# Two chained matmuls per expert: computing the first one also by quarters in seven products, with the sums of its input kept in DRAM

## The chip, the cores and the metric

The kernel runs on 1 core of one Trainium2 chip. The metric is device time in microseconds (us). Before the change it took 1112.87 us (median of 3 runs, 1112.77 to 1113.21). Every run below that is called fast ran at a mean granted TensorE clock of 0.98 or more in its records. Single runs, whose state cannot be told, are marked.

Engines: PE is TensorE (PEld: its weight loads, which overlap its matmuls: 693.4 us of loads beside 1072.2 us of matmuls in the 1108.5 us of the kernel before), DVE is VectorE, ACT is ScalarE, POOL is GpSimd, SP issues DMA transfers (POOL issues some of them too). The order of each engine's instructions is laid down when the kernel is built, and the traces show the engines keeping to it (in a run below ACT did 19 operations in a row, 11.75 us, while PE waited for one behind them). The program keeps a plan of operations with estimated durations, orders them, and issues them engine by engine.

## The reference, cut to what matters

```python
def _attn_ref(q, k, v, w_phi):     # a linear attention; 8 x 8 heads of 576 rows, 64 wide
    ...
def _moe_ref(x, w_gate, w1, w2):   # x: 4608 x 512, 8 experts, F = 1024
    P = np.exp(x @ w_gate - max)
    for _ in range(8):             # routing: normalise rows and columns in turn, 8 times
        P /= P.sum(1, keepdims=True) + 1e-09
        P /= P.sum(0, keepdims=True) + 1e-09
        P *= N / E
    for e in range(E):
        h = np.maximum(x @ w1[e], 0.0)      # "up":   512 -> 1024
        out += P[:, e:e+1] * (h @ w2[e])    # "down": 1024 -> 512
    return out
```

The rows of x are worked on in 9 groups of 512. Expert 0 is computed beside the attention and the routing, because its products need no `P`. Experts 1 to 7 follow: 63 expert-groups of one up and one down.

## The kernel before

Down of experts 1 to 7 is already computed by quarters. Each matrix is cut into 2 x 2 blocks, and the block product is formed from seven block products instead of eight, at the price of sums of blocks. Four sums of the activations (`S`) are made for every group, two on POOL and two on DVE. Four sums of the weights (`T`) are made once per expert on POOL.

```python
def up(w1, g, hT, fcs, n, r=(), w=()):           # plain: 8 blocks of four 512-column matmuls
    for f0 in fcs[::n]:
        ph = new(f"P{n}")
        ...   pe(512, ... mm(ph..., w1()[:, dc, f*128:(f+1)*128], xT[:, dc, g*512:(g+1)*512], ...))
        act(512 * n, ... nc.scalar.activation(out=hT..., in_=ph..., func=ACT.Relu ...))

def sums_w(w2):                                  # once per expert, on POOL
    T = new("T")
    for n, x, y, r in ((0, b[0,1], b[0,0], []), (1, b[1,1], lambda: t(0), [0]), ...):
        pool(1024, lambda: nc.gpsimd.tensor_tensor(out=t(n), in0=x(), in1=y(), op=ALU.subtract), ...)

def down7(e, g, hT, w2, T):
    add(pool, 2, lambda: a(0, 0), lambda: a(1, 0), ALU.subtract, hk[0])     # S sums of a group
    add(dve,  0, lambda: a(1, 0), lambda: a(1, 1), ALU.add, ...)
    add(dve,  1, lambda: S[0](), lambda: a(0, 0), ALU.subtract, ...)
    add(pool, 3, lambda: a(0, 1), lambda: S[1](), ALU.subtract, ...)
    ...                                          # seven products of eight 256-column matmuls
    if e == 1:                                   # expert 0's share of acc gets its gate value
        for ts in range(4):
            act(512, ... nc.scalar.activation(out=acc[g][:, ts, :], in_=acc[g][:, ts, :],
                func=ACT.Copy, scale=P[:, 4*g + ts, 0:1]), ...)
    # six products are read by DVE:          acc = P_e * bank + acc   (two per product)
    # one is scaled by ACT into U and added by POOL:  acc = acc + U

for e in range(1, E):
    w1, w2 = load_w(e, ...)
    T = sums_w(w2)
    for g in ...:
        hT = new("hT"); up(w1, g, hT, ...); down7(e, g, hT, w2, T)
```

Of the kernel before, what the change touches and what calls it, by code (L numbers as in the profile page):

```python
# [41 lines left out]
class Op:  # L42
    __slots__ = ("eng", "dur", "lat", "nbytes", "fn", "left", "ready", "users", "idx", "end",
                 "bufs", "deps")
# [8 lines left out]
class Plan:  # L53
# [3 lines left out]
    def __init__(self):  # L57
        self.last, self.readers = {}, {}
        self.ops = []
        self.prio = 0  # L60

    def op(self, eng, dur, lat, fn, r=(), w=(), takes=(), nbytes=0):

        o = Op()
        o.eng, o.dur, o.lat, o.fn, o.nbytes = eng, dur, lat, fn, nbytes
        o.users, o.idx, o.end, o.ready = [], len(self.ops) + self.prio, None, 0.0
        deps = {}
        for key in r:
            for d in self.last.get(key, ()):
                deps[id(d)] = d  # L70
        for key in w:
            for d in list(self.last.get(key, ())) + self.readers.get(key, []):
                deps[id(d)] = d
        bufs = list(takes)
        for key in list(r) + list(w):
            b = key[0] if isinstance(key, tuple) else key
            if isinstance(b, Buf):
                bufs.append(b)
        o.bufs = list({id(b): b for b in bufs}.values())
        for b in o.bufs:  # L80
            b.left += 1
        for key in r:
            self.readers.setdefault(key, []).append(o)
        for key in w:
            self.last[key] = [o]
            self.readers[key] = []
        o.deps = list(deps.values())
        o.left = len(o.deps)
        for d in o.deps:
            d.users.append(o)  # L90
        self.ops.append(o)
        return o

    def start(self, o, free):

        t = max(free, o.ready)
# [11 lines left out]
    def schedule(self):  # L108
# [7 lines left out]
        while len(done) < len(self.ops):  # L116
# [17 lines left out]
            free[o.eng] = at + o.dur  # L134
            if o.nbytes:
# [27 lines left out]
def kernel(  # L163
# [33 lines left out]
    ps = ctx.enter_context(tc.tile_pool(name="ps", bufs=1, space=PSUM))  # L197

    ident = const.tile([128, 128], BF16, name="ident")
    wphi_f = const.tile([128, DF], FP32, name="wphi_f")  # L200
    wphi2 = const.tile([128, 2, DF], BF16, name="wphi2")
    wphi2f = wphi2.rearrange("p a b -> p (a b)")
# [9 lines left out]
    a_in = tc.alloc_tile_pool(name="a_in", bufs=1)  # L212

# [15 lines left out]
    def dve(el, fn, r=(), w=()):  # L229
        plan.op("DVE", el / 960.0 + 0.09, 0.22, fn, r, w)  # L230

    def pool(el, fn, r=(), w=()):
        plan.op("POOL", el * 1.64e-3 + 0.17, 0.25, fn, r, w)
# [13 lines left out]
    ring(hp, [128, 8, 512], BF16, "hT", 2)  # L247
# [22 lines left out]
    ring("s_p", [128, 4, 4, 256], BF16, "T", 2)  # L270
    ring("s_p", [128, 4, 256], BF16, "S", 8)
    ring("s_p", [128, 2, 256], FP32, "U", 2)
    ring("s_p", [128, NT, E], FP32, "u", 1)
    ring("s_p", [128, NT, E], FP32, "wv", 1)
# [14 lines left out]
    def load_w(e, r=()):  # L289
        w1, w2 = new("w1"), new("w2")  # L290
        dma("POOL", 2 << 20, 280, lambda: nc.gpsimd.dma_start(  # L291
            out=w1(), in_=moe_w1[e].rearrange("(c p) f -> p c f", p=128)),
            r, [(w1, i) for i in range(4)])
        dma("POOL", 2 << 20, 280, lambda: nc.gpsimd.dma_start(
            out=w2(), in_=moe_w2[e].rearrange("(c p) f -> p c f", p=128)),
            r, [(w2, i) for i in range(4)])
# [350 lines left out]
    def up(w1, g, hT, fcs, n, r=(), w=()):  # L647

        for f0 in fcs[::n]:
            ph = new(f"P{n}")  # L650
            for i in range(n):
                for dc in range(NP):
# [3 lines left out]
                        xkeys(g, dc) + [(w1, (f0 + i) // 2), *r], [ph, *w], [hT])  # L656
            act(512 * n, lambda f0=f0, ph=ph: nc.scalar.activation(  # L657
                out=hT()[:, f0:f0 + n, :].rearrange("p a b -> p (a b)"),
                in_=ph()[:, 0:512 * n], func=ACT.Relu, bias=0.0, scale=1.0),
                [ph], [(hT, f0 + i) for i in range(n)])  # L660

    def down(w2, hT, tss, r=()):
        py = new(f"P{len(tss)}")
        for i, ts in enumerate(tss):
            for fc in range(8):
                pe(512, lambda i=i, ts=ts, fc=fc: mm(
                    py()[:, 512 * i:512 * i + 512], hT()[:, fc, ts * 128:(ts + 1) * 128],
                    w2()[:, fc, :], fc == 0, fc == 7),
                    [(hT, f) for f in (range(8) if fc == 0 else (fc,))]
# [8 lines left out]
    def up0(g, part):  # L678
        if part == 0:
            hts[g] = new("hT")  # L680
# [53 lines left out]
    LAG = 6  # L734
# [82 lines left out]

    def routing():
        c_bc = None
        for it in range(8):  # L820
            rr, wv, cs, pc = new("rr"), new("wv"), new("cs"), new("P1")
# [5 lines left out]
            else:  # L827
                u = new("u")
                uk = [u]
# [7 lines left out]
                out=wv(), in0=L, in1=rr()[:, :, None].to_broadcast([128, NT, E]),  # L837
                op=ALU.mult), lk + [rr], [wv])
            dve(480, lambda wv=wv, cs=cs: nc.vector.tensor_reduce(
                out=cs(), in_=wv().transpose([0, 2, 1]), axis=AX.X, op=ALU.add), [wv], [cs])  # L840
# [6 lines left out]
            out=P, in0=wv(), in1=c()[:, None, :].to_broadcast([128, NT, E]), op=ALU.mult),  # L847
# [22 lines left out]
    def sums_w(w2):  # L870

        b = {(i, j): (lambda i=i, j=j: w2()[:, 4 * i:4 * i + 4, 256 * j:256 * j + 256])
             for i in range(2) for j in range(2)}
        T = new("T")

        def t(n):
            return T()[:, n]

        wk = [(w2, i) for i in range(4)]
        for n, x, y, r in ((0, b[0, 1], b[0, 0], []), (1, b[1, 1], lambda: t(0), [0]),  # L880
                           (2, b[1, 1], b[0, 1], []), (3, b[1, 0], lambda: t(1), [1])):
            pool(1024, lambda n=n, x=x, y=y: nc.gpsimd.tensor_tensor(
                out=t(n), in0=x(), in1=y(), op=ALU.subtract),
                wk + ["late"] + [(T, i) for i in r], [(T, n)])
        return T

    def down7(e, g, hT, w2, T):



        def a(i, j):
            return hT()[:, 4 * j:4 * j + 4, 256 * i:256 * i + 256]

        def b(i, j):
            return w2()[:, 4 * i:4 * i + 4, 256 * j:256 * j + 256]

        S = [new("S") for _ in range(4)]
        hk = [[(hT, f) for f in range(4 * j, 4 * j + 4)] for j in range(2)]
        wk = [(w2, i) for i in range(4)]

        def add(eng, n, x, y, op, r):
            f = nc.vector if eng is dve else nc.gpsimd
            eng(512 if eng is dve else 1024,
                lambda: f.tensor_tensor(out=S[n](), in0=x(), in1=y(), op=op), r, [S[n]])  # L904

        add(pool, 2, lambda: a(0, 0), lambda: a(1, 0), ALU.subtract, hk[0])
        add(dve, 0, lambda: a(1, 0), lambda: a(1, 1), ALU.add, hk[0] + hk[1])
        add(dve, 1, lambda: S[0](), lambda: a(0, 0), ALU.subtract, [S[0]] + hk[0])
        add(pool, 3, lambda: a(0, 1), lambda: S[1](), ALU.subtract, [S[1]] + hk[1])

        def product(bank, lhs, rhs, r, first):
            for i in range(2):
                for k in range(4):
                    z = i == 0 and k == 0
                    pe(256, lambda i=i, k=k, z=z: nc.tensor.matmul(  # L915
                        bank()[:, 256 * i:256 * i + 256], lhsT=lhs()[:, k, 128 * i:128 * i + 128],
                        rhs=rhs()[:, k, :], start=first and z, stop=k == 3,
                        skip_group_check=True), r + wk + (["P"] if z else []), [bank])
# [10 lines left out]

        if e == 1:  # L930
# [6 lines left out]
        product(y, lambda: a(0, 1), lambda: b(1, 0), hk[1], True)  # L937
        read(y, 0, 0)
        product(x, lambda: a(0, 0), lambda: b(0, 0), hk[0], True)
        u = new("U")  # L940
        for n in range(2):
            act(256, lambda n=n: nc.scalar.activation(
                out=u()[:, n, :], in_=x()[:, 256 * n:256 * n + 256], func=ACT.Copy, bias=0.0,
                scale=P[:, 4 * g + n, e:e + 1]), [x, "P"], [(u, n)])
        pool(512, lambda: nc.gpsimd.tensor_tensor(  # L945
            out=acc[g][:, 0:2, 0:256], in0=acc[g][:, 0:2, 0:256], in1=u(), op=ALU.add),
            [(u, 0), (u, 1)], [("acc", g, n, 0) for n in range(2)])
        product(z, lambda: S[0](), lambda: T()[:, 0], [S[0], (T, 0)], True)
        read(z, 1, 1)
        product(x, lambda: S[1](), lambda: T()[:, 1], [S[1], (T, 1)], False)  # L950
        read(x, 0, 1)
        product(x, lambda: S[2](), lambda: T()[:, 2], [S[2], (T, 2)], False)
        read(x, 1, 1)
        product(z, lambda: S[3](), lambda: b(1, 1), [S[3]], False)
        read(z, 0, 1)
        product(x, lambda: a(1, 1), lambda: T()[:, 3], hk[1] + [(T, 3)], False)
        read(x, 1, 0)

    for e in range(1, E):
        w1, w2 = load_w(e, [("xT", 5, 3)])  # L960
        T = sums_w(w2)
        for g in (list(range(NG)) if e < E - 1 else [8] + list(range(8))):
            hT = new("hT")
            up(w1, g, hT, range(8), 1, r=["up0"])
            plan.prio = 100
            down7(e, g, hT, w2, T)
            plan.prio = 0
            if e == E - 1:
                for ts in range(4):
                    store(g, ts)  # L970
    plan.run(tc)
# [30 lines left out]
```

## Time and profile before

| what | value | view |
|---|---|---|
| profiled span | 1108.5 us, clock 0.995 | cores |
| PE busy | 97% | page, part 1 |
| share of PE in the chain that ended last | 86% | page, part 4 |
| period of a middle group | 13.02 us, PE busy throughout | windows |
| an expert of nine groups (experts 2 to 6) | 118.0 to 118.3 us | timeline |
| up of a group | 8 x 0.867 = 6.93 us | timeline |
| down of a group | 7 x 0.868 = 6.08 us | timeline |

These lines of the page before give the busy time of each engine with its share of the span and number of instructions, and the shares of the chain of work that ended last.

```profile
PE 1072.2 (97%) x8024; PEld 693.4 (63%) x8024; DVE 637.6 (58%) x1422; ACT 579.9 (52%) x1190; POOL 565.1 (51%) x520
...
PE 86%; ACT 5%; DVE 4%; issue 1%; POOL 0%; DVEq 0%; ACTq 0%
```

The windows view of the kernel before, over two periods of a middle group, lists the stretch, its length, busy time and number of instructions of PE, PEld, DVE, ACT and POOL, the granted clock, the DMA share and GB/s.

```profile
599.70:612.72 13.02, 13.02 (x90) 8.62 (x89) 6.35 (x15) 5.61 (x11) 5.46 (x3) 1.00 0.00 1
612.72:625.74 13.02, 13.02 (x90) 8.60 (x89) 6.36 (x15) 5.61 (x11) 6.27 (x4) 1.00 0.22 35
```

PE is busy for the whole period, and DVE, ACT and POOL for less than half of it. A change here is worth what it takes from PE, as long as the other engines keep up.

The PE timeline of the kernel before (start, length, engine, line, operation, number) shows two up blocks and two down products.

```profile
601.58 1.03 PE L379 MATMUL P_8440<-xT,w_6228 128*128 128x512 bf16 x4
602.44 1.03 PE L379 MATMUL P_8448<-xT,w_6228 128*128 128x512 bf16 x4
...
609.26 1.04 PE L915 MATMUL P_8408<-w_6457,S 128*128 128x256 bf16 x8
610.13 1.04 PE L915 MATMUL P_8366<-T,S 128*128 128x256 bf16 x8
```

Blocks overlap in this view (1.03 us long, but 0.86 us apart), so the spacing of starts is what counts: 0.86 us for four 512-column matmuls (about 216 ns each) and 0.87 for eight 256-column ones (108.5 ns).

The timeline of the kernel before at an expert boundary (DVE and POOL) shows the one thing that disturbs it there.

```profile
543.15 2.11 POOL L882 TENSOR_TENSOR T<-w_7654 128x1024 bf16<-128x1024 bf16 x1
543.68 2.13 DVE L904 TENSOR_TENSOR S<-hT 128x1024 bf16<-128x1024 bf16 x1
545.23 2.56 POOL L882 TENSOR_TENSOR T<-w_7654,T 128x1024 bf16<-128x1024 bf16 x1
```

The DVE sum, which takes 0.68 us when nothing disturbs it, took 2.13 us while POOL summed weights. This cost PE a wait of 0.66 us. It recurs every 118 us, and is the boundary cost of the kernel before.

### The profile page before, as it was taken

To read this page: it belongs to the slowest core of one execution; us is meant where nothing else is said; L and a number is where in the kernel's file an instruction comes from. 1 tells how busy PE (TensorE), PEld (TensorE's weight loads), DVE (VectorE), ACT (ScalarE), POOL (GpSimd) and SP (SyncE) were. 2 spreads that over 40 slices of the span, in tenths; PEclk is the share of its full clock that TensorE was granted. 3 is DMA by queue.
4 is the path that set the end of the run, shared out by engine and by line. 5 is a ranking of instruction groups with operands and counts; after the bars stand their busy time and mean duration, and the time that the engine had idled before them with its cause. 6 is when DMAs were issued, how large, how long until landed. Compare 5 with 4: busy or idle time off the path is not lost.

```text
span 1108.5 us, 20141 instructions
## 1 busy us (share of the span) xinstructions
PE 1072.2 (97%) x8024; PEld 693.4 (63%) x8024; DVE 637.6 (58%) x1422; ACT 579.9 (52%) x1190; POOL 565.1 (51%) x520
## 2 busy tenths in 40 slices
PE   5889999999999999999999999999999999999997
PEld 3556666644566666666666666666666666666665
DVE  6889888883445555444545555444545555444455
ACT  6799899927744444444444444444444444444442
POOL 8775655530743447444743474445644474444433
PEclk9999999999999999999999999999999999999999
DMA  9997978402100040002200220022000400002112
GB/s 157 154 175 117 152 127 153 70 1 47 31 1 1 5 73 1 1 1 40 38 1 1 39 39 1 1 39 38 1 1 2 75 2 1 1 1 76 77 77 114
DMA packets 84189, 53.52 MB, mean 48 GB/s; under 512 B 43008, under 2 KB 77952, under 8 KB 84096
## 3 DMA queue, kind: packets, MB, share of 16 engines
q0 software_dynamic: 40080, 26.23, 17.6%
q1 hardware_dynamic: 44016, 26.02, 10.0%
q8 instruction: 62, 1.02, 0.4%
q14 instruction: 31, 0.25, 0.1%
HBM read 61.95 MB, written 9.44 MB: 64 GB/s over the span
## 4 chain that ended last, share of the span: by engine, by line
PE 86%; ACT 5%; DVE 4%; issue 1%; POOL 0%; DVEq 0%; ACTq 0%
DVE acc_79 L924 1%; ACT hT L657 1%; DVE S L904 1%; PE P_5334 L915 0%; PE P_13295 L915 0%; PE P_13027 L915 0%; PE P_10496 L915 0%; PE P_9961 L915 0%; PE P_7970 L915 0%; PE P_6773 L915 0%; PE P_6238 L915 0%; PE P_12759 L915 0%; PE P_12625 L915 0%; PE P_12353 L915 0%; PE P_12221 L915 0%
## 5 line engine op out<-in xcount | busy, mean ns | idle before, releaser
L904 POOL TENSOR_TENSOR S<-hT,S 128x1024 bf16<-128x1024 bf16 x63 | 133.9, 2125 | 284.8 <-DVE S L904 284.8
L915 PEld LDWEIGHTS <-S 128*128 128x128 bf16 x2016 | 197.5, 98 | 38.3 <-issue 1.4
L904 POOL TENSOR_TENSOR S<-hT 128x1024 bf16<-128x1024 bf16 x63 | 133.5, 2118 | 102.2 <-ACT hT L657 102.2
L915 PEld LDWEIGHTS <-hT 128*128 128x128 bf16 x1512 | 148.1, 98 | 25.2 <-issue 5.6
L904 DVE TENSOR_TENSOR S<-hT 128x1024 bf16<-128x1024 bf16 x63 | 51.9, 824 | 14.0 <-ACT hT L657 14.0
L379 PEld LDWEIGHTS <-w_3836 128*128 128x128 bf16 x288 | 28.2, 98 | 32.3
L379 PEld LDWEIGHTS <-w_11016 128*128 128x128 bf16 x288 | 28.2, 98 | 32.0
L379 PEld LDWEIGHTS <-w_7425 128*128 128x128 bf16 x288 | 28.2, 98 | 32.1
L379 PEld LDWEIGHTS <-w_6228 128*128 128x128 bf16 x288 | 28.2, 98 | 32.1
L379 PEld LDWEIGHTS <-w_9819 128*128 128x128 bf16 x288 | 28.2, 98 | 32.1
L379 PEld LDWEIGHTS <-w_8622 128*128 128x128 bf16 x288 | 28.1, 98 | 32.1
L379 PEld LDWEIGHTS <-w_5074 128*128 128x128 bf16 x288 | 28.1, 98 | 32.1
L904 DVE TENSOR_TENSOR S<-S,hT 128x1024 bf16<-128x1024 bf16 x63 | 47.6, 756 | 0.0
L379 PEld LDWEIGHTS <-hT 128*128 128x128 bf16 x288 | 28.1, 101 | 26.3 <-issue 2.3
L379 PEld LDWEIGHTS <-w_429 128*128 128x128 bf16 x288 | 25.8, 98 | 23.5 <-issue 2.1
L379 PEld LDWEIGHTS <-qkT 128*128 128x128 bf16 x256 | 23.5, 98 | 17.6 <-DVE xb_r L590 4.2
L291 POOL DMA_DIRECT2D w_5074<-in_moe_w_dram x1 | 0.8, 823 | 29.0 <-PE P_5064 L379 29.0
L319 POOL DMA_DIRECT2D qk<-in_k_dram x17 | 13.5, 795 | 2.2 <-issue 1.1
L319 POOL DMA_DIRECT2D qk<-in_q_dram x17 | 13.0, 767 | 0.0
L604 PEld LDWEIGHTS <-xb 128*128 128x128 bf16 x128 | 8.0, 97 | 3.4 <-issue 1.7
L945 POOL TENSOR_TENSOR acc_78<-acc_78,U 128x512 f32<-128x512 f32 x7 | 9.3, 1330 | 0.0
L452 PEld LDWEIGHTS <-qk 128*128 128x128 bf16 x64 | 4.5, 102 | 7.5 <-DMA qk<-in_k_dram 4.9
(3730 smaller groups left out, 2979.2 us busy)
## 6 DMA issues: line engine op xcount, KB each, us to landing
v_m<-in_v_dram SPq DMA_DIRECT2D x15, 512.0 KB, 5.1
qk<-in_k_dram POOLq DMA_DIRECT2D x15, 256.0 KB, 5.5
qk<-in_q_dram POOLq DMA_DIRECT2D x15, 256.0 KB, 6.2
w_429<-in_moe_w_dram POOLq DMA_DIRECT2D x4, 256.0 KB, 7.0
w_988<-in_moe_w_dram POOLq DMA_DIRECT2D x4, 256.0 KB, 9.2
w_3836<-in_moe_w_dram POOLq DMA_DIRECT2D x1, 1024.0 KB, 10.7
w_3851<-in_moe_w_dram POOLq DMA_DIRECT2D x1, 1024.0 KB, 16.5
w_5074<-in_moe_w_dram POOLq DMA_DIRECT2D x1, 1024.0 KB, 8.1
```

The lines of the kernel that those rows point to most:

```text
L291: dma("POOL", 2 << 20, 280, lambda: nc.gpsimd.dma_start(out=w1(), in_=moe_w1[e].rearrange("(c p) f -> p c f", p=128)), r, [(w1, i) for i i ...
L319: dma("POOL", nh << 17, 230, lambda x=x, src=src: nc.gpsimd.dma_start(out=t["qk"]()[:, x, o:o + nh], in_=src[b, hh:hh + nh, 0:SM].rearrang ...
L379: nc.tensor.matmul(out_, lhsT=lhsT, rhs=rhs, start=start, stop=stop)
L452: pe(128, lambda x=x, c=c, ptr=ptr: nc.tensor.transpose(bf(ptr)[:, c * 128:(c + 1) * 128], t["qk"]()[:, x, h0 + c // 2, (c % 2) * 128:(c % ...
L604: pe(128, lambda j=j: nc.tensor.transpose(bf(pxt)[:, j * 128:j * 128 + 128], xb()[:, j, :], ident), [(xb, 0), (xb, 1), "ident"], [pxt])
L657: act(512 * n, lambda f0=f0, ph=ph: nc.scalar.activation(out=hT()[:, f0:f0 + n, :].rearrange("p a b -> p (a b)"), in_=ph()[:, 0:512 * n], ...
L904: lambda: f.tensor_tensor(out=S[n](), in0=x(), in1=y(), op=op), r, [S[n]])
L915: pe(256, lambda i=i, k=k, z=z: nc.tensor.matmul(bank()[:, 256 * i:256 * i + 256], lhsT=lhs()[:, k, 128 * i:128 * i + 128], rhs=rhs()[:, k ...
L924: dve(350, lambda n=n, ts=ts: nc.vector.scalar_tensor_tensor(out=acc[g][:, ts, 256 * j:256 * j + 256], in0=bank()[:, 256 * n:256 * n + 256 ...
L945: pool(512, lambda: nc.gpsimd.tensor_tensor(out=acc[g][:, 0:2, 0:256], in0=acc[g][:, 0:2, 0:256], in1=u(), op=ALU.add), [(u, 0), (u, 1)], ...
```

## The change

The intent is to save an eighth of the up matmuls as well. Up becomes 7 block products for each of two halves of the features, 14 products of four 256-column matmuls: 56 x 108.5 ns = 6.08 us instead of 6.93. In return:

- Four more weight sums per expert (eight in all) run on POOL. Two of them are made in place in the weight buffer.
- Sums of xT are needed in every group of every expert. They are computed once, in expert 1, stored to DRAM, and loaded for each group (two transfers of 256 KB).
- Up results are now sums of several banks: ACT copies a bank to SBUF (`U`), and DVE adds another bank to it with a saturating add that also does the relu. There are six such adds a group, where ACT alone did the relu before.
- To make room on DVE, four products per group go through ACT and POOL instead of one; in return all four `S` sums go to DVE.
- The order of the products of up (of this group) and down (of the last group) is written out and fixed. Buffers and `LAG` (6 to 7) are adapted.

```diff
@@ sums of the weights: eight instead of four, on POOL @@
-    def sums_w(w2):
+    def sums_w(w1, w2):
+        sub(pool, 1024, s(2), q(w1, *a11), q(w1, *a21), ALU.subtract, ... + late, [S[2]])
+        sub(pool, 1024, q(w1, *a21), q(w1, *a21), q(w1, *a22), ALU.add, ...)      # in place
+        sub(pool, 1024, s(1), q(w1, *a21), q(w1, *a11), ALU.subtract, ...)
+        sub(pool, 1024, s(3), q(w1, *a12), s(1), ALU.subtract, ...)
+        ...  # the same four for w2
@@ sums of xT: computed once, kept in DRAM @@
+    def sums_x(g):
+        X = [new("X") for _ in range(2)]
+        ...  sub(dve, 512, x(n), y, z, ALU.subtract, ...)                          # four
+        for i in range(2):
+            dma("SP", 1 << 18, 250, lambda i=i: nc.sync.dma_start(out=Xd[g][i], in_=X[i]()), ...)
+    def load_x(g):
+        ...  dma("SP", 1 << 18, 250, lambda i=i: nc.sync.dma_start(out=X[i](), in_=Xd[g][i]), ...)
@@ up by quarters @@
+    def up7(A, g, X, hT, r0):
+        def keep(fp, n):   act(512, lambda: nc.scalar.copy(out=u[fp][n]()..., in_=x[fp]()), ...)
+        def add(bank, fp, n, i, j):
+            dve(660, lambda: nc.vector._custom_dve(ADD_SAT, out=out_(fp, i, j),
+                in0=bank[fp]()..., in1=u[fp][n](), s0=3.0e38, s1=0.0), ...)
+        ...  # x1 y1 x2 w1 x3 x4 w2, each for fp = 0 and 1
@@ down7: all S sums on DVE; four products through ACT and POOL @@
-        add(pool, 2, ...)   add(pool, 3, ...)
+        sub(dve, 1024, lambda: S[2](), ...)   sub(dve, 1024, lambda: S[3](), ...)
+        def read2(bank, i, j):
+            ...  act(256, ... scale=P...)  twice;  pool(512, ... acc = acc + u)
@@ the loop @@
+    ORDER = "X1 x10 x11 y11 w11 x21 x20 w10 x31 y10 w21 x30 X2 x41 x40 Z1 X3 w20 X4 Z2 Y1".split()
     for e in range(1, E):
         w1, w2 = load_w(e, [("xT", 5, 3)])
-        T = sums_w(w2)
+        if e == 1:
+            for g in range(NG):
+                sums_x(g)
+        A7, B7 = sums_w(w1, w2)
         for g in ...:
+            X = load_x(g)
+            ...  # the products of ORDER: up7 of this group, down7 of the last one
```

## The prediction

> **What bounds the kernel now.** The page gives PE 97% of 1108.5 us; the chain of waits is 86% PE. In the timeline the expert phase (63 expert-groups, about 272 to 1100 us) repeats every 13.0 us without gaps: 8 up blocks of four 512-column matmuls, 0.867 us each (6.93), then 7 down products of eight 256-column matmuls, 0.868 us each (6.08). Windows over one period: PE 13.00, DVE 6.3, ACT 5.6, POOL 5.5 us. Long chain entries recur every 118.0 us, so an expert boundary costs 118.0 - 9 x 13.0 = about 1 us (a DVE sum of 2.1 to 2.5 us). Attention and routing hardly change.
>
> **What the change removes.** Up becomes 14 products of four 256-column matmuls: 56 x 108.5 ns = 6.08 us instead of 6.93. That is 0.86 us per group, 54 us in all. The weight load (98 ns) stays hidden below 108.5 ns. All of it is on the critical path while PE stays gap-free.
>
> **What it adds per group,** from durations of the trace:
> - DVE: six PSUM adds of 128x512 (estimate 0.7 us, from 0.68 us for PSUM copies of 512) = 4.2; four sums instead of two, 4 x 0.68 = 2.7; six accumulates x 0.44 = 2.6. Sum 9.5 of 12.15 us.
> - ACT: 8 x 0.60 + 8 x 0.42 = 8.2 us.
> - POOL: four f32 adds x 1.27 = 5.1 us; its two sums of 2.12 go to DVE.
> - DMA: 512 KB of x sums, some 43 GB/s, on nearly idle queues.
>
> So PE still bounds a steady group, in a tight order with DVE near 80%. I expect 0.1 to 0.4 us of PE waits per group, nearer the first.
>
> **Where the gain is lost.**
> 1. Expert boundaries. POOL does eight weight sums (2.12 to 2.4 us each) instead of four. In its in-order queue they stand between the adds, and one waits for a weight load of 8 to 10 us: about 16 us of POOL work in a 12 us group. [...]I expect 2 to 5 us per boundary, six boundaries: 20 us.
> 2. Expert 1 computes, stores and reloads the x sums through three shared buffers: 4 us. Routing's multiplications, slowed by the POOL sums, hide under expert 0.
> 3. The first group has no down product beside it, the last no up: 3 us.
>
> Sum: -54 + 6 (steady waits) + 14 (boundaries, beyond today's 6) + 4 + 3 = -27 us.
>
> **Prediction: 1086 us,** 8 in 10 between 1060 and 1107. Faster by over 2%: 0.66; within 2%: 0.30; slower: 0.04.
>
> **What would show each step.** Right: a middle group's period of 12.2 to 12.5 us in the timeline; expert matmuls (1 to 7) of 256 columns; DVE 75 to 85% busy in such a window; adds of 0.7 us; 112 to 116 us from expert to expert, with PE gaps in the groups around each boundary that end on POOL weight sums, or on ACT or DVE behind them. Wrong: 12.8 or more in middle groups, with PE waiting for "hT", "U" or bank reads.
>
> **What would make it wrong.** The custom add at half rate (DVE over 12 us, no gain); POOL adds and DVE sums blocking each other in every group; x loads late behind stores in the SP queue; or, to the other side, boundaries as smooth as today (about 1065).

The trace of before does show DVE sums of 2.1 to 2.5 us beside POOL's weight sums, where they take 0.68 us alone.

## The result, and the profile after

The changed kernel is correct and took 1095.61 us (median of 4 fast runs, 1094.63 to 1095.97) against 1112.82 us for the kernel before (4 fast runs, 1112.63 to 1113.21). The ratio is 0.984, 95% interval 0.983 to 0.986. Ratios here are the mean time of one kernel's fast runs over that of the other's in the same rounds, so they are not quite the ratio of the medians quoted. The profiled span went from 1108.5 to 1094.2 us: 14.3 us less, at clocks of 0.995 and 0.996. (The medians differ by 17.2 us. The profiled run of the kernel before took 1110.51 us, 2.3 us under its median, so the comparison by spans below shows a little less gain.)

The same two lines of the page after:

```profile
PE 1027.8 (94%) x9498; PEld 841.6 (77%) x9536; DVE 885.0 (81%) x1584; ACT 707.9 (65%) x1568; POOL 626.0 (57%) x611
...
PE 69%; DVE 10%; POOL 9%; ACT 7%; issue 4%; DMA 1%; ACTq 0%; DVEq 0%; POOLq 0%
```

PE lost 44 us of work, yet the span only 14. The chain says where to look: 26% of it is now on DVE, POOL and ACT, where it was 9%. The windows of two middle groups of the kernel after:

```profile
566.44:578.66 12.22, 12.22 (x114) 10.96 (x112) 10.01 (x17) 7.60 (x17) 5.50 (x4) 1.00 0.15 44
578.66:590.89 12.23, 12.23 (x114) 10.96 (x112) 9.82 (x17) 7.61 (x17) 5.51 (x4) 1.00 0.14 44
```

In the middle of an expert the change does what was intended. The period is 12.22 us against 13.02, without PE gaps, and with DVE at 80 to 82%. The loss must lie elsewhere, and the timeline shows where: in the seven stretches from one expert's first up matmul to the next one's.

| stretch | before, us | after, us | after, if every group took 12.22 | lost after |
|---|---|---|---|---|
| start to expert 1 | 272.81 | 278.14 | | +5.3 against before |
| expert 1 | 117.93 | 121.09 | 104.1 (*) | 17.0 |
| expert 2 | 118.02 | 113.25 | 110.0 | 3.3 |
| experts 3 to 6, each | 118.0 to 118.3 | 114.8 to 115.3 | 110.0 | 4.8 to 5.3 |
| expert 7 to the last matmul | 122.67 | 116.90 | 116.1 | 0.8 |

(*) This stretch holds nine ups but only eight downs: its 959 matmuls at 108.5 ns make 104.1 us.

The boundary of experts 2 and 3 in the timeline of the kernel after:

```profile
526.98 2.13 POOL L896 TENSOR_TENSOR w_8312<-w_8312 128x1024 bf16<-128x1024 bf16 x1
...
528.28 4.68 DVE L896 TENSOR_TENSOR S<-S,hT 128x1024 bf16<-128x1024 bf16 x1
...
529.07 1.26 POOL L1100 TENSOR_TENSOR acc_4740<-acc_4740,V 128x512 f32<-128x512 f32 x1
...
530.29 2.11 POOL L896 TENSOR_TENSOR T<-w_8312 128x1024 bf16<-128x1024 bf16 x1
...
532.88 0.68 DVE L1015 CUSTOM_DVE_ANT_0 hT<-P_8596,U 128x512 bf16<-128x512 f32 x1
...
534.21 0.60 PE L983 MATMUL P_8573<-xT,T 128*128 128x256 bf16 x4 [2.03 <-DVE hT L1015]
```

Read it from the end. PE waited 2.03 us for an add of DVE. That add stood in DVE's queue behind one `S` sum that took 4.68 us instead of 0.68. The sum starts while POOL runs a weight sum (526.98 to 529.11), and ends only when POOL's whole run of three back-to-back operations is over (532.40). The same wait of 2.03 us stands at 648.98, 763.75 and 879.06. The step from expert 6 to 7 is a control that the kernel itself contains: there is no expert 8 whose `w1` sums would follow, so only four weight sums run there instead of eight. It has no such wait, and the whole last stretch lost 0.8 us.

The groups view of the kernel after gives the mean of the three kinds of `S` sum (busy time, mean ns), which was 824 and 756 ns before (the two kinds that DVE made):

```profile
L896 DVE TENSOR_TENSOR S<-hT 128x1024 bf16<-128x1024 bf16 x126 | 110.3, 907 | 4.0 <-ACT hT L1020 3.9
L896 DVE TENSOR_TENSOR S<-S,hT 128x1024 bf16<-128x1024 bf16 x63 | 75.7, 1201 | 0.4
L896 DVE TENSOR_TENSOR S<-hT,S 128x1024 bf16<-128x1024 bf16 x63 | 65.8, 1044 | 0.2
```

The boundaries are only part of this rise. The median `S` sum took 0.88 us, against 0.68 before, and in the two middle groups above, where POOL made no weight sums but only its adds of `acc`, the sums took 0.68 to 1.13 us. There it cost PE nothing.

The start to expert 1 got longer in the routing. The timeline of the kernel after (DVE, POOL, PE):

```profile
234.69 2.36 DVE L844 TENSOR_TENSOR T<-L,c_bc 128x288 f32<-128x288 f32 x1
236.69 2.34 POOL L896 TENSOR_TENSOR w_3852<-w_3852 128x1024 bf16<-128x1024 bf16 x1
...
240.19 0.36 PE L384 MATMUL P_4851<-cs,colw 128*128 128x8 f32 x2 [2.10 <-DVE cs L853]
...
244.68 0.39 PE L384 MATMUL P_4887<-cs,colw 128*128 128x8 f32 x2 [1.09 <-DVE cs L853]
...
249.63 0.36 PE L384 MATMUL P_4927<-cs,colw 128*128 128x8 f32 x2 [1.09 <-DVE cs L853]
```

Expert 1's weight sums now run on POOL during the routing. A multiplication of routing that takes 0.46 us alone took 2.36. The small matmuls of routing stand at fixed places in PE's queue, so PE waits for them (2.10 + 1.09 + 1.09 = 4.3 us) although matmuls of expert 0 stand behind. Before, the longest such wait was 0.67 us.

### The profile page after: what moved, and what is told of

It reads as the page before. It is cut to its first block, busy times and chain, and to the rows that moved or that the text cites. A ratio compares the mean times of both kernels' runs of the same rounds, so it can differ in the third digit from the quotient of the medians.

```text
span 1094.2 us, 24560 instructions
## 1 busy us (share of the span) xinstructions
PE 1027.8 (94%) x9498; PEld 841.6 (77%) x9536; DVE 885.0 (81%) x1584; ACT 707.9 (65%) x1568; POOL 626.0 (57%) x611
## 4 chain that ended last, share of the span: by engine, by line
PE 69%; DVE 10%; POOL 9%; ACT 7%; issue 4%; DMA 1%; ACTq 0%; DVEq 0%; POOLq 0%
DVE S L896 3%; POOL T L896 3%; POOL acc_4739 L1100 2%; DVE hT L1015 1%; ACT V L1097 1%; POOL acc_4740 L1100 1%; DVE m L376 1%; ACT U L1011 1%; POOL acc_77 L1100 1%; DVE X L896 1%; DMA qk_r<-in_q_dram 1%; DVE xb L590 0%; POOL acc_79 L1100 0%; PE P_6476 L983 0%; DVE T L844 0%
## 5 line engine op out<-in xcount | busy, mean ns | idle before, releaser
L983 PEld LDWEIGHTS <-T 128*128 128x128 bf16 x1512 | 148.0, 98 | 33.5 <-issue 16.0
L896 DVE TENSOR_TENSOR S<-hT 128x1024 bf16<-128x1024 bf16 x126 | 110.3, 907 | 4.0 <-ACT hT L1020 3.9
L896 DVE TENSOR_TENSOR S<-S,hT 128x1024 bf16<-128x1024 bf16 x63 | 75.7, 1201 | 0.4
L1100 POOL TENSOR_TENSOR acc_78<-acc_78,V 128x512 f32<-128x512 f32 x28 | 38.6, 1385 | 53.1 <-ACT V L1097 47.6
L1100 POOL TENSOR_TENSOR acc_80<-acc_80,V 128x512 f32<-128x512 f32 x28 | 38.0, 1360 | 51.0 <-ACT V L1097 44.2
L1100 POOL TENSOR_TENSOR acc_81<-acc_81,V 128x512 f32<-128x512 f32 x28 | 38.1, 1362 | 49.8 <-ACT V L1097 49.2
L896 DVE TENSOR_TENSOR S<-hT,S 128x1024 bf16<-128x1024 bf16 x63 | 65.8, 1044 | 0.2
L1100 POOL TENSOR_TENSOR acc_79<-acc_79,V 128x512 f32<-128x512 f32 x28 | 38.4, 1373 | 47.9 <-ACT V L1097 44.0
L1100 POOL TENSOR_TENSOR acc_4738<-acc_4738,V 128x512 f32<-128x512 f32 x28 | 38.0, 1360 | 48.3 <-ACT V L1097 47.8
L1100 POOL TENSOR_TENSOR acc_4737<-acc_4737,V 128x512 f32<-128x512 f32 x28 | 38.0, 1360 | 48.0 <-ACT V L1097 44.0
L1100 POOL TENSOR_TENSOR acc_77<-acc_77,V 128x512 f32<-128x512 f32 x28 | 37.1, 1336 | 25.8 <-ACT V L1097 25.3
L1100 POOL TENSOR_TENSOR acc_4740<-acc_4740,V 128x512 f32<-128x512 f32 x28 | 39.8, 1430 | 13.6 <-ACT V L1097 9.8
L384 PEld LDWEIGHTS <-w_449 128*128 128x128 bf16 x288 | 26.1, 99 | 22.8 <-issue 2.9
L1100 POOL TENSOR_TENSOR acc_4739<-acc_4739,V 128x512 f32<-128x512 f32 x28 | 37.7, 1352 | 5.7 <-DVE acc_4739 L1087 4.5
L983 PEld LDWEIGHTS <-w_3831 128*128 128x128 bf16 x288 | 28.2, 98 | 4.7 <-issue 1.1
L983 PEld LDWEIGHTS <-w_5134 128*128 128x128 bf16 x288 | 28.2, 98 | 3.4 <-issue 0.2
L983 PEld LDWEIGHTS <-w_8312 128*128 128x128 bf16 x288 | 28.2, 98 | 3.3
L983 PEld LDWEIGHTS <-w_6801 128*128 128x128 bf16 x288 | 28.2, 98 | 3.3
```

Of the source, the lines that this page charges most:

```text
L384: nc.tensor.matmul(out_, lhsT=lhsT, rhs=rhs, start=start, stop=stop)
L896: lambda: f.tensor_tensor(out=out_(), in0=x(), in1=y(), op=op), r, w, **kw)
L983: pe(256, lambda i=i, k=k, z=z: nc.tensor.matmul(bank()[:, 256 * i:256 * i + 256], lhsT=lhs(k, i), rhs=rhs(k), start=first and z, stop=k = ...
L1100: pool(512, lambda: nc.gpsimd.tensor_tensor(out=acc[g][:, 2 * i:2 * i + 2, 256 * j:256 * j + 256], in0=acc[g][:, 2 * i:2 * i + 2, 256 * j: ...
```

## The experiments

My theories after the result were: (L) the boundaries are lost to weight sums on POOL that block DVE sums (POOL reads SBUF while DVE wants two inputs from it: beside POOL's weight sums in the trace of after, 18 `S` sums took 1.06 to 4.68 us, while 65 of DVE's adds and 44 of its accumulates, with an input from PSUM, took 0.67 to 0.69 and 0.47 to 0.48 us as elsewhere), and run back to back; (R) the late start is the same block in routing; (X) expert 1's loss comes from work that only expert 1 does: sums of xT, their stores and loads, and the scaling of `acc` by expert 0's gate values. The main rival was that the new steady load (DVE 81%) leaves too little slack, so that order and placement would not matter. All twelve kernels give correct results except where said. All edits are against the changed kernel ("after").

### All sums of xT stored before any is loaded

```diff
-    def load_x(g):
+    def load_x(g, hold=()):
...
-                [("Xd", g, i)], [X[i], "order of X"])
+                [("Xd", g, i), *hold], [X[i], "order of X"])
...
-            X = load_x(g)
+            X = load_x(g, [("Xd", n, i) for n in range(NG) for i in range(2)] if e == 1 else [])
```

> One change to the changed kernel: no x sum is loaded back before all eighteen have been stored, so that all 36 DVE subtractions run beside expert 0 and routing instead of inside expert 1. The result stays right. Theory X (expert 1's 17 us of loss come from making the x sums inside its groups: DVE work and buffers that loads and stores share): expert 1 takes 108 to 112 us instead of 121.1, the whole 1084 to 1090 us. Rival W (the loss is expert 1's own scaling of acc by P on ACT and the accumulation order, or the missing down product of its first group): expert 1 stays at 117 to 121 us. Expert 1 starts up to 3 us later in both.

Measured: 1097.78 us (1097.18 to 1100.81), ratio to before 0.987 (0.985 to 0.989): no gain over after. In its PE timeline the many waits of expert 1 became one, and expert 1 then ran without gaps until its last groups:

```profile
296.52 1.44 PE L983 MATMUL P<-X,w 128*128 128x256 bf16 x6 [12.25 <-DMA X<-xd]
```

The windows view of the same kernel (PE alone, then clock, DMA share, GB/s) shows a second cost of so long a wait:

```profile
284.00:296.50 12.50, 0.27 (x3) 0.63 0.94 209
296.50:298.50 2.00, 1.98 (x10) 0.50 0.45 145
298.50:300.50 2.00, 2.00 (x11) 0.50 0.00 0
300.50:310.00 9.50, 9.29 (x84) 0.98 0.30 84
```

After the wait the granted clock stood at 0.50 for about 4 us, in which PE did 21 matmuls, where 108.5 ns each would give 37. What follows: the sums of xT are indeed part of expert 1's loss, but collecting them into one block in front only moved the loss. This was a miss as an improvement, and a step toward one: the wait is now in one place, where it can be filled.

### Expert 1's weight sums after the routing

```diff
+        if e == 1:
+            g8 = new("g8")
+            pool(8, lambda: nc.gpsimd.tensor_copy(out=g8(), in_=P[:, 0, :]), ["P"], [g8, "go"])
-        A7, B7 = sums_w(w1, w2)
+        A7, B7 = sums_w(w1, w2, ["go"] if e == 1 else [])      # each sum also reads "go"
```

> One change to the changed kernel: POOL first copies eight values of P, so that its eight weight sums of expert 1 start after routing (about 262 us) instead of at 228 us. The result stays right. Theory R (the 4.3 us of PE waits for routing's column sums, 240 to 250 us, come from POOL sums that block DVE's multiplications of two SBUF inputs): those waits go to under 1 us, routing's multiplications take 0.46 us each throughout, expert 1 starts 3 to 4 us earlier (274 to 275 us). Rival S (the waits come from the x subtractions put between routing's steps on DVE): they stay at 3 to 4 us. Against it: the held sums may come late for expert 1's first products, some us lost again there. Whole: 1090 to 1097 us.

Measured: 1102.62 us (1100.83 to 1104.95), ratio 0.992 (0.990 to 0.994). The waits for `cs` in routing are gone, so theory R is right about their cause. But expert 1, into which the sums now fall, took 129.3 us instead of 121.1, with waits of 1.5 to 2.3 us for ACT and DVE: it lost more than routing gained, and the whole is 7 us slower than after, outside the expected 1090 to 1097. That the sums there are the cause is not shown: with clears in place of the sums (below) expert 1 took as long.

### The next expert's w1 sums in the middle of an expert

```diff
-        late = ["late"]
+        late = ["late", *hold]
...
-        A7, B7 = sums_w(w1, w2)
+        A7, B7 = sums_w(w1, w2, [("acc", 3, 2, 1)] if e > 1 else [])   # the four w1 sums only
```

> One change to the changed kernel: the four POOL sums of the next expert's first weights wait until group 3 of the present expert is accumulated; only the four sums of the second weights stay at the expert boundary. Nothing is removed. The result stays right. Theory P (eight POOL sums crowded into two groups at each boundary cost about 5 us[...]): experts 3 to 6 take 111 to 112.5 us instead of 115, the 2.03 us PE wait on DVE hT at the start of the second group goes, whole 1075 to 1084 us. Rival M (the loss is the switch of weights itself: new weight buffers, loads of the weights, x loads): experts stay at 114 to 115 us, whole 1093 to 1097 us.

Measured: 1090.22 us (1089.89 to 1090.48), ratio 0.980 (0.979 to 0.982). Experts 3 to 5 took 111.65 us each instead of about 115, and the waits of 2.03 us are gone. The number and the work of the sums are unchanged, so their placement makes the boundary cost. The whole missed the expected 1075 to 1084 us, since expert 1 took about 7 us longer than in after (128.3 us, with one PE wait of 4.10 us for ACT). Four sums for expert 2 now fell into its groups, but that this is the reason is not shown: expert 1 also took 128 to 129 us in the next three runs, wherever the sums lay.

### Sums replaced by operations that only write

Each sum is replaced by two clears of the same tile, which take about as long (3.87 us for four, so 1.9 against 2.1 to 2.4) but read nothing. The result is wrong (relative error 1.08).

```diff
+    def clr(out_, x, y, op, r, w):
+        for _ in range(2):
+            pool(512, lambda: nc.gpsimd.memset(out_(), 0.0), r, w)
-        sub(pool, 1024, s(2), ...)
+        clr(s(2), ...)                                   # and so for all eight
```

> Wrong result on purpose: each POOL weight sum is replaced by two POOL clears of the same tile, which occupy POOL's in-order queue but read no SBUF. Theory L[...]: no DVE sum takes over 2.2 us at a boundary, where one took 4.7 us, and experts 3 to 6 take under 112.5 us. Rival Q (what hurts is only POOL's queue: the adds to acc stand behind the sums and hold up ACT and the banks): with clears of about 1 us each, some 16 us of POOL work stay and experts take 113.5 us or more. If the clears are much shorter than 1 us each, Q is not excluded by this run.

Measured: 1082.67 us (one run, state unknown). Experts 3 to 5 took 111.45 to 111.56 us, as theory L expected, and the longest wait at their boundaries was 0.34 us; the waits in routing were gone too. (Its clock was 0.992, and it is 12.0 us under the lowest of after's four runs, which lie within 1.3 us of each other.) Expert 1 did not gain: it took 128.8 us, nearly 8 more than in after. Its timeline at a boundary, DVE and POOL:

```profile
527.49 3.87 POOL L901 MEMSET T<- 128x1024 bf16 x4
...
529.24 0.67 DVE L896 TENSOR_TENSOR S<-S,hT 128x1024 bf16<-128x1024 bf16 x1
```

A DVE sum ran in 0.67 us in the midst of four clears, where in after one took 4.68 us across three POOL operations that read SBUF. POOL's time at the boundary is not the cost; its reading of SBUF is.

### The same sums in halves (a control)

A rival to the last reading is that clears help by being short. Here each sum is cut into two that still read.

```diff
+    def two(out_, x, y, op, r, w):
+        for i in range(2):
+            sub(pool, 512, part(out_, i), part(x, i), part(y, i), op, r, w)
-        sub(pool, 1024, s(2), ...)
+        two(s(2), ...)                                   # and so for all eight
```

> Control for the run with clears: the changed kernel with each POOL weight sum cut into two sums of half the columns, about 1.1 to 1.2 us each, 16 per expert, so POOL's operations have the length and number of the clears but read SBUF as the originals do. Correct result. Theory L[...]: DVE sums of over 2 us at the boundary stay, experts 3 to 6 take 113.5 to 116 us, as with whole sums (115), against 111.4 with clears. Rival G (the clears helped because they were short, so that adds to acc slipped between them): experts take 111 to 112.5 us here too.

Measured: 1128.0 us (one run, state unknown, clock 0.979), 32 us slower than after. An expert took 119.5 us. Its timeline at a boundary (POOL, DVE, PE):

```profile
540.45 7.68 DVE L896 TENSOR_TENSOR S<-hT 128x1024 bf16<-128x1024 bf16 x2
...
541.29 1.26 POOL L1113 TENSOR_TENSOR acc<-acc,V 128x512 f32<-128x512 f32 x1
...
542.52 2.25 POOL L896 TENSOR_TENSOR T<-w 128x512 bf16<-128x512 bf16 x2
...
544.74 2.25 POOL L896 TENSOR_TENSOR T<-w,T 128x512 bf16<-128x512 bf16 x2
...
549.46 0.58 PE L996 MATMUL P<-X,w 128*128 128x256 bf16 x2 [5.87 <-ACT U L1024]
```

Two DVE sums took 7.68 us where they take 1.4, and PE waited 5.87 us for a copy of ACT, which itself waited 5.92 us for an add that stood behind these sums on DVE. Shorter operations did not help, so the rival falls. Nor is a DVE sum sure to come next when one POOL operation ends. The first of the two sums here waited through six POOL operations that followed each other without a pause, as the one of 4.68 us in after did through three. Other sums got in between two such operations. One stands in the timeline of after (POOL, DVE):

```profile
516.43 2.12 POOL L896 TENSOR_TENSOR T<-w_6928,T 128x1024 bf16<-128x1024 bf16 x1
517.11 1.99 DVE L896 TENSOR_TENSOR S<-hT,S 128x1024 bf16<-128x1024 bf16 x1
...
518.51 2.57 POOL L896 TENSOR_TENSOR T<-w_8312 128x1024 bf16<-128x1024 bf16 x1
```

Here DVE came next, and POOL's following sum took 2.57 us instead of 2.12. What decides between the two cases is not shown. But where POOL paused, even for 0.08 us, no waiting DVE sum was passed over in the traces of before and after (55 places with a pause of 0.08 us in after; each sum ended about 0.55 us after the POOL operation before the pause). So what helps is a pause of POOL after each sum, not a shorter sum.

### One sum per group

From the last three runs follows the placement: one sum after each of groups 1 to 6, and only two at the boundary. A tenth buffer for sums makes room.

```diff
-    ring("s_p", [128, 1024], BF16, "T", 9)
+    ring("s_p", [128, 1024], BF16, "T", 10)
+        def at(n):
+            return [("acc", n, 2, 1)] if e > 1 else []
-            k(w1, *a11) + k(w1, *a21) + late, [S[2]])
+            k(w1, *a11) + k(w1, *a21) + late + at(1), [S[2]])
...                                          # at(2) to at(6) for the next five sums
```

> The changed kernel with one POOL weight sum of the next expert per group, behind the accumulations of groups 1 to 6, only the last two at the boundary (a tenth buffer for sums makes that possible). Correct result. Theory P (crowding of POOL sums at the boundary): experts 3 to 6 take 110.3 to 111.5 us, less than the 111.65 of the four-and-four split; expert 1, already short of time, is not helped or loses up to 5 us. Whole 1080 to 1088 us. Rival: the remaining loss is the switch itself, experts stay at 111.5 to 112 us.

Measured: 1083.87 us (1083.51 to 1084.31), ratio 0.975 (0.973 to 0.976). One expert takes 110.63 us, against nine periods of 12.22 = 110.0. What is left of the boundary is one wait, in the PE timeline:

```profile
515.89 1.03 PE L987 MATMUL P<-T,hT 128*128 128x256 bf16 x8 [0.43 <-ACT V L1101]
...
626.52 1.03 PE L987 MATMUL P<-T,hT 128*128 128x256 bf16 x8 [0.43 <-ACT V L1101]
```

So theory L accounts for the boundaries, and the rival (no slack at a DVE load of 80%) falls for experts 2 to 7. Expert 1 took 128.3 us and has two waits of 2.98 us.

### One sum per group, and all sums of xT first

This joins the first experiment and the last, and gives the xT sums of groups 6 to 8 to POOL.

```diff
-            sub(dve, 512, x(n), y, z, ALU.subtract, ...)
+            sub(pool if g in (6, 7, 8) else dve, 512, x(n), y, z, ALU.subtract, ...)
```

> The spread weight sums, and all x sums stored before any is loaded, as in the run that did so alone, with the x sums of groups 6 to 8 made on POOL, and no POOL sums for expert 2 in the way of the last x subtractions (they took 2.2 us each there, and PE waited 12.2 us for the first load). Correct result. Theory X: the 12.2 us wait falls to 0 to 5 us, expert 1 then runs without gaps near 12.2 us per group, experts 2 to 6 at 110.3 to 111.5 us, whole 1066 to 1078 us, faster than both kernels. If the wait for the loads stays at 10 us or more, the three buffers and their stores bound it, and the whole stays at 1078 to 1086 us.

Measured: 1080.51 us (1078.0 to 1084.23), ratio 0.972 (0.970 to 0.974). Expert 1 runs gap-free after its start, but it began at 285.3 us (7 later than in after, with four waits in routing of 5.7 us in sum), and the start has one PE wait of 14.6 us for the first load of xT sums. In front of it, a sum of xT waited 7.13 us for a store to leave its buffer. Better than the last by 3 us only. Theory X was not met; the wait of over 10 us and the time fall under the expectation's other case (1078 to 1086 us), in which the three buffers and their stores bound the start.

### The lag of expert 0 as before

```diff
-    LAG = 7
+    LAG = 6
```

> The changed kernel with expert 0 starting at the lag of 6 of the kernel before instead of 7. Rival T for the start (expert 1 begins 5.3 us later because the longer lag leaves more of expert 0 behind attention): expert 1 begins near 273 to 275 us. Theory R (it begins later because PE waits in routing for sums blocked by POOL): the attention phase ends 1 to 2 us later or earlier, the waits for routing's column sums stay at 3.5 to 4.5 us in sum, and expert 1 begins at 277 to 279 us. Whole within 3 us of 1095.

Measured: 1096.83 us (one run, state unknown). Expert 1 starts as late as in after, and the waits for `cs` stand (1.40, 1.10 and 1.10 us). The lag is not the cause of the late start.

### Group 0's xT sums used from SBUF

This builds on the run before the last: weight sums one per group, xT sums all stored first, but all made on DVE again. The sums are made in the order 1 to 8, 0, and group 0, with which expert 1 begins, uses its sums where they were made. The first load is then needed one group later.

```diff
-            for g in range(NG):
-                sums_x(g)
+            for g in [*range(1, NG), 0]:
+                X0 = sums_x(g)                            # returns X, all sums on DVE again
...
-            X = load_x(g)
+            X = X0 if e == 1 and g == 0 else load_x(g, ...)      # the rest waits for all stores
```

> As the run with spread sums and x sums first, but: all x sums on DVE again, made in the order of groups 1 to 8 and then 0, and expert 1's first group reads its sums where they were made instead of loading them back. The load of expert 2's weights is issued as before, near 277 and 286 us. Correct result. Theory X (PE waited 14.6 us for sums that came late through three buffers): the wait falls to 2 to 8 us, whole 1068 to 1076 us. Theory D (the late stores of x sums, one of which held a DVE subtraction for 7.1 us, queue behind the 4 MB weight load[...]): a store that falls into the weight load still takes over 5 us, and the wait stays at 5 to 8 us.

Measured: 1074.62 us (1073.63 to 1075.03), ratio 0.966 (0.965 to 0.968). The whole is in the range of theory X, but the long wait at the start of expert 1 is longer than expected (10.58 us), and now it is for ACT. Its timeline (ACT and PE):

```profile
280.69 11.75 ACT L1112 ACTIVATE acc<-acc,P 128x512 f32<-128x512 f32 x19
...
292.32 1.07 ACT L1016 COPY U<-P 128x512 f32<-128x512 f32 x2
...
292.96 1.01 PE L988 MATMUL P<-X,T 128*128 128x256 bf16 x4 [10.58 <-ACT U L1016]
```

ACT ran 19 scalings of `acc` in a row ahead of the first copy that PE was waiting for. None of these scalings was urgent: those of group 8 are needed some 100 us later. They stand there because the plan holds nothing that keeps them back. In after the same 36 scalings lie between 265.9 and 296.7 us, among the first copies.

### Expert 2's weights later

The load of expert 2's weights shares the start of expert 1 with the stores of xT sums (in the last kernel it is issued at 270.1 and 278.7 us, the stores from 246.8 to 286.6 us). Here it is held until group 0 is accumulated, on top of the last kernel.

```diff
-        w1, w2 = load_w(e, [("xT", 5, 3)])
+        w1, w2 = load_w(e, [("acc", 0, 0, 0)] if e == 2 else [("xT", 5, 3)])
```

> The run above with one change: expert 2's weights are loaded only after the first group of expert 1 is accumulated (its spread sums then come in groups 2 to 6). Correct result. Theory D: no store of x sums takes over 4 us any more, the first group's wait is 2 to 5 us shorter than in the run above, whole 1065 to 1073 us. Rival: the stores were late for their own chain of three buffers; then both runs have the same wait within 1 us and the same time.

Measured: 1078.06 us (1077.62 to 1078.86), ratio 0.970 (0.968 to 0.972). The late store is gone (the longest DVE wait for a store fell from 3.47 to 0.59 us), but it was not what ended last: PE still waits 11.27 us for ACT. The sums had to start a group later, two fell into group 6, and an expert took 111.27 us. A net loss of 3.4 us: theory D's time was missed, and the rival has the wait right (within 1 us of the run above) but not the time.

### The scalings of acc held, alone

```diff
-                    scale=P[:, 4 * g + ts, 0:1]), ["P", ("acc", g, ts)],
+                    scale=P[:, 4 * g + ts, 0:1]), ["P", ("acc", g, ts)]
+                    + ([("acc", g - 3, 1, 0)] if g > 3 else []),
```

> The changed kernel with one edit: ScalarE's scaling of acc by expert 1's gate value, for groups 4 to 8, waits until expert 1 has accumulated the group three before it, instead of all 36 scalings running in a row at the start of expert 1. Theory A (the 36 in-order scalings, 0.6 to 0.7 us each, stand ahead of expert 1's copies and are a large part of the 17 us that expert 1 loses): expert 1 takes 115 to 119 us instead of 121.1, the rest stays at 113 to 115 us each, whole 1090 to 1094 us. Rival (expert 1 is short of ScalarE and VectorE time in total, with 2.8 us of scalings added to 8.2 us of other ScalarE work in a group of 12.2 us, so the order does not matter): expert 1 stays within 2 us of 121, whole 1094 to 1098 us. Routing and the boundaries of experts 2 to 6 should not move under either.

(The expectation says "expert 1's gate value". That is a slip: the scaling is by expert 0's, `P[:, ..., 0:1]`.)

Measured: 1097.23 us (1096.36 to 1097.57), ratio 0.987 (0.985 to 0.988). The two expectations split. Expert 1 took 118.7 us, in theory A's range (2.4 us less than in after), but the whole kernel is in the rival's range, as expert 2 took about 115.5 us instead of 113.25 (the same wait in expert 3 stands at 520.08 in this kernel and at 519.75 in after). The timeline at the start of expert 2 (POOL and ACT) shows what was lost there:

```profile
421.18 2.57 POOL L896 TENSOR_TENSOR T<-w,T 128x1024 bf16<-128x1024 bf16 x1
...
423.71 1.71 POOL L1100 TENSOR_TENSOR acc<-acc,V 128x512 f32<-128x512 f32 x1
...
425.45 0.84 ACT L1097 ACTIVATE V<-P,P 128x256 f32<-128x256 f32 x2 [3.36 <-POOL acc L1100]
```

The last weight sum stood between POOL's adds of `acc`, and ACT waited 3.36 us for one of these adds; PE's two waits for ACT there were 1.74 and 1.73 us. By itself the edit is worth nothing: the time that it saved in expert 1 was lost again in expert 2. I can show where the time was lost again, but not why the planned order at that boundary turned out worse than after's.

### The scalings held, in the best kernel so far

The same edit on top of the kernel with group 0 used from SBUF.

> The fastest kernel so far (sums of the weights spread one per group, all sums of xT stored before expert 1's loads, group 0 used directly from SBUF at the end of expert 1; 1074.6 us) with the same hold on the scalings of acc. Theory A: the 10.6 us wait of the first U copies for ScalarE at the start of expert 1 falls under 3 us; whole 1064 to 1071 us. Rival: ScalarE is then too full in expert 1's groups and the time is lost again in waits of 1 to 2 us spread over the groups; whole 1072 to 1078 us.

(The expectation says that group 0 is used "at the end of expert 1". That is a slip: it is made last among the sums and used first.)

Measured: 1068.35 us (1067.65 to 1069.23), ratio 0.961 (0.959 to 0.963), correct. In its PE timeline the long wait has shrunk from 10.58 to 2.75 us and is no longer for ACT:

```profile
286.48 1.30 PE L988 MATMUL P<-X,T 128*128 128x256 bf16 x8 [2.75 <-DVE X L896]
288.08 1.86 PE L988 MATMUL P<-X,w 128*128 128x256 bf16 x8 [0.30 <-ACT U L1016]
...
293.02 0.61 PE L988 MATMUL P<-X,w 128*128 128x256 bf16 x4 [0.97 <-DMA X<-xd]
```

Expert 1 takes 112.4 us, where it took 119.0 in the kernel without this edit and 121.1 in after. The rival (ACT too full in expert 1) falls: with the other waits gone, the same scalings fit in later. This is the fastest kernel, 44 us below before and 27 us below after by the medians.

## Why the prediction was right, and where its terms were not

The time lies inside the range (1060 to 1107), 9.6 us above the predicted 1086. The likeliest of the three outcomes, faster by over 2%, did not come: the ratio of 0.984 falls in "within 2%", which had a chance of 0.30. The sum, term by term, each measured on the profiled spans:

| term | predicted, us | measured, us | from |
|---|---|---|---|
| PE work removed, 63 x (13.02 - 12.15) | -54 | -54.8 | periods of the timeline |
| waits in steady groups | +6 | +4.4 | 63 x (12.22 - 12.15) |
| boundaries | +20 (six) | +23.3 (five, in experts 2 to 6) | table of stretches |
| losses of the kernel before | -6 | -10.7 | 831.0 - 63 x 13.02 in the expert phase |
| expert 1 | +4 | +17.0 (with the sixth boundary and the first group) | table of stretches |
| first and last group | +3 | +0.8 (the last alone) | expert 7 |
| routing slowed | 0 | +5.3 (4.3 of it waits in routing, about 1 already at the end of the attention) | start of expert 1 |
| tail | 0 | +0.2 | end of the span |
| sum | -27 | -14.5 (the spans differ by 14.3) | |

- **"PE still bounds a steady group ... DVE near 80%": right.** The period is 12.22 us, gap-free, DVE 81%, and the add took 0.68 to 0.69 us for an estimate of 0.7. This was the step with the largest risk, and it held to 0.07 us per group. The block of POOL's adds and DVE's sums, which the prediction feared in every group, does occur (`S` sums of 0.68 to 1.13 us for the 0.68 of the prediction), but DVE still fits: 9.8 to 10.0 us busy, for 9.5 predicted.
- **"Expert boundaries": the place and the cause (POOL's weight sums, and DVE sums slow beside them) were right, with one detail wrong.** The size was 3.3 to 5.3 us for 2 to 5 predicted. Clears in place of sums removed the loss, halves made it worse, and one sum per group removed it with the sums intact. The detail "one waits for a weight load of 8 to 10 us" did not show: POOL's sums followed one another directly. In its place, a DVE sum could wait through a whole run of POOL operations (4.68 us) and not through one of them (2.1), which the prediction did not have.
- **"Expert 1 computes, stores and reloads the x sums ...: 4 us": the term that was mis-sized most.** It measured 17.0 us, of which the prediction had perhaps 4 plus one boundary of 3.3 plus part of the 3 for the first group. It left out that DVE and ACT are already well loaded in a group when the xT sums (about 22 us of DVE) and the 36 scalings of `acc` (0.6 to 0.7 us each, about 23 us of ACT) come on top, and that all of these stand early in in-order queues. Spreading the weight sums, ordering the xT sums, using group 0's directly and holding the scalings took expert 1 from 121.1 to 112.4 us. Experiment by experiment the parts do not add: holding the scalings brought 6.3 us with the rest in place and nothing by itself.
- **"Routing's multiplications, slowed by the POOL sums, hide under expert 0": wrong.** PE waited 4.3 us for them. The step forgot that the small routing matmuls have fixed places in PE's queue, so that expert 0's matmuls behind them cannot fill the wait. Moving the sums behind the routing, or replacing them by clears, removed the waits.
- **The losses of the kernel before were larger than said** (10.7 for 6): its expert 1 also lost about 4 us, which the prediction did not look at. That error went the other way, and offset 4.7 us of the rest.

The total came into the range although the gain was little more than half of the -27 by spans; without the larger losses of the kernel before it would have been smaller still.

What stays open: expert 1 took 128 to 129 us in the five runs that moved, cut, cleared or spread the weight sums and left the xT sums alone, 7 to 8 more than in after, and no run shows why; 8 us are still lost in expert 1 of the best kernel, of which the PE waits above and the half clock near them (0.50 from 287.4 to 290.0 us) are part; the 4.3 us of routing waits are still there, since the one cure tried cost more than it gave; and the loss at the start of expert 2 with the scalings held alone is located but not explained.

## What to carry to other kernels

Cutting the work of the bounding engine paid in full in the steady state here, with the next busiest engine (DVE) at 80 to 82%. Look for the price where one-off work (weight sums, first-use sums, rescaling) meets that tighter steady state: here, net of what the kernel before already lost in these places, it ate about 36 of 55 us. Spread one-off work on POOL so that it pauses after each operation that reads SBUF (one sum per group took an expert from about 115 to 110.63 us), and hold back work on in-order queues that is ready early but needed late (PE's long wait fell from 10.58 to 2.75 us). A wait removed alone may buy nothing until the waits beside it are gone too, so try fixes together before discarding one.

## What the runs show of the hardware

- A DVE sum that waits for POOL can be passed over by further POOL operations that follow without a pause: one of 0.68 us took 4.68 us across three POOL operations (after), and two took 7.68 us across six of about 1.1 to 1.3 us each (sums in halves). In other places a DVE sum got in after the first (1.99 us, after). What decides is not shown.
- After PE waits of 5.87 us (sums in halves), 10.58 us (group 0 from SBUF) and 12.25 us (the first experiment) the clock stood at 0.50, for about 4 us in the first experiment; after a single wait of 2.03 us (after) it stood at 1.00. Shorter waits were followed by it too: one of 2.75 us by 0.50 (the fastest kernel), and one of 2.98 us, in a stretch where PE had been busy for 2.3 of 5.8 us, by 0.53 (one sum per group, expert 1). In the first experiment PE did 21 matmuls in those 4 us, where 108.5 ns each would give 37, so I estimate the cost at nearly 2 us on top of the wait.
- The saturating add with one PSUM and one SBUF input, 128x512, took 0.67 to 0.69 us (after), about the same as a sum of two 128x1024 bf16 tiles in SBUF that nothing disturbed (0.68, before). Four POOL clears of a 128x1024 bf16 tile took 3.87 us (the run with clears), a POOL sum of two such tiles 2.12 us (before).
